# Other tiles for one block's sums, and an output whose stores are joined in pairs: a delta-rule attention with two dense layers on one core

## The chip, the core and the metric

The kernel runs on one core of one Trainium2 chip. The core has a matrix engine (TensorE, PE in the profile), three engines for elementwise work (VectorE or DVE, ScalarE or ACT, GpSimd or POOL), a SyncE (SP) that in this kernel only issues DMA transfers, and 16 DMA engines that carry the transfers. Each engine works through its own instructions in order and waits on semaphores for the others. The metric is the device time of one execution in microseconds; less is better. Three runs of the kernel before took 1066.85, 1068.50 and 1068.76 us (median 1068.5).

## The reference, cut to what matters

```python
def _attn_ref(q, k, v, beta):                  # (4, 8, 768, 48) each, beta (4, 8, 768)
    k_n = k / (norm(k) + 1e-6)
    for t in range(S):
        y[:, :, t] = q_t @ state
        state += b_t * outer(k_t, v_t - state.T @ k_t)

x = attn_out.transpose(0, 2, 1, 3).reshape(B * S, H * D)     # 3072 tokens x 384
h = x @ w_in;  x = elu(h) @ w_out                            # 384 -> 2048 -> 384, "layer 1"
h = x @ w2_in; x = (h * sigmoid(1.702 * h)) @ w2_out         # the same again, "layer 2"
```

The result is the float32 matrix of 3072 tokens by 384, token index `b * 768 + s`.

## The kernel before, in words

The 768 positions are cut into six blocks of 128 (p = 0 to 5, NP = 6). A block holds 128 positions of the four batches, 512 tokens (TB). The attention works in twelve chunks of 64 positions, two for each block, and is woven into the dense layers' loop.

The main loop in `schedule` has 192 units: layer 1 ("t") block by block with 16 units each (one unit is one slice of 128 of the 2048 hidden columns), then layer 2 ("n") in the same way. In a unit `up` (L573) makes nine matmuls into one PSUM bank `h`; ScalarE and VectorE apply the activation and split the result in a high and a low part, `gh` and `gl`; two units later (LAG = 2) `down_t` (L607, nine matmuls of 512 columns) or `down_n` (L618, twelve of 384) multiplies them by the second weight into accumulators in PSUM that stay open for the block's 16 units. Other work (attention steps, the conversion of the weights, the loading of the next block) hangs on tables `mid`, `end` and `fill` by unit number, which fixes every engine's order in the program text.

At the end of a block of layer 1, `end_t` copies the three accumulators (`acc`, 128 x 512 each) into two tiles of 128 x 768, `xo`: VectorE copies accumulator 0 and half of 1 into the first (L673), ScalarE accumulator 2 and the other half of 1 into the second (L671). SP stores both to a scratch tensor in DRAM, `x1d` (L653, L654). The next block's `down_t` needs the same three banks. A tile's tag names a ring of buffers: the tiles `xo` of blocks 0 to 4 have the tag "w" of pool `mp`, two buffers in all; those of block 5 the tag "xo" of pool `w2p`, also two. The ring "w" serves the weight conversion as well: each 128-row slice of weights comes as 64-bit words (`raw`, L527), ScalarE rescales them (L531), VectorE makes 32-bit words `w` of them (L538, L541), and ScalarE and VectorE split those in a high and a low part `wt` (L548, L552). The conversion of layer 2's weights runs through blocks 4 and 5 of layer 1. Pool `w2p` is opened in `attention_done`, in unit 79, the last of block 4; the sums of block 4 are copied out two units later.

In layer 2 a block begins with `x1_load`: SP loads `x1r` (768 KB) from `x1d` (L629), ScalarE (L634) and GpSimd (L635) split it in `xh` and `xl`. That is done one block ahead, in the units 2 to 12 of the block before. At a block's end `end_n` copies four accumulators (128 tokens x 384 each, w = 0 to 3) into tiles `on`, VectorE those of w = 0 and 2, ScalarE those of w = 1 and 3; each tile holds 64 positions of two batches, one batch in partitions 0 to 63, the other in 64 to 127, so it goes to two places in the output, 768 rows apart.

Of the kernel before, what the change touches and what calls it, by code (L numbers as in the profile page):

```python
# [17 lines left out]
B, H, S, D = 4, 8, 768, 48  # L18
DM = H * D
DFF = 2048  # L20
P = 128
NP = S // P
# [9 lines left out]
class Kernel:  # L32
# [607 lines left out]

    def end_t(self, p, c0, n, acc):

        pool, tag = (self.w2p, "xo") if p == NP - 1 else (self.mp, "w")
        d = self.x1d[p]
        halves = [pool.tile([P, 2 * DM], F32, name="xo", tag=tag, bufs=2) for _ in range(NK * n // (2 * DM))]
        if n == TB:
            x, y, n2 = *halves, n // 2
            self.evac(0, x[:, 0:n], acc[0])
            self.evac(1, y[:, n2:n2 + n], acc[2])
            self.evac(0, x[:, n:], acc[1][:, 0:n2])  # L650
            self.evac(1, y[:, 0:n2], acc[1][:, n2:n])
            d = d.rearrange("p k t -> p (k t)")
            self.nc.sync.dma_start(d[:, 0:2 * DM], x)  # L653
            self.nc.sync.dma_start(d[:, 2 * DM:], y)  # L654
        else:
            x = halves[0].rearrange("p (k t) -> p k t", k=NK)
            for c in range(NK):
                self.evac(c, x[:, c], acc[c])
            self.nc.sync.dma_start(d[:, :, c0:c0 + n], x)

    def end_n(self, p, acc):
        for w in range(NW):
            o = self.w2p.tile([P, DM], F32, name="on", tag="on", bufs=4)
            self.evac(w, o, acc[w])
            for ab in range(2):
                r = (2 * (w % 2) + ab) * S + p * P + 64 * (w // 2)
                self.nc.sync.dma_start(self.out[r:r + 64, :], o[64 * ab:64 * ab + 64])

    def evac(self, i, out, in_):
        if i % 2:  # L670
# [361 lines left out]
```

## Time and profile before

| what | value |
|---|---|
| median of the runs | 1068.5 us (1066.85 to 1068.76) |
| the profiled execution | 1067.46 us, of which the profile's span 1065.8 us |
| TensorE busy | 1001.8 us, 94% of the span |
| VectorE, ScalarE, GpSimd busy | 590.9, 451.4, 49.1 us |
| DMA | 68.41 MB, mean 64 GB/s |
| mean granted TensorE clock | 0.981 |

The span runs from the first to the last instruction of the profiled execution; 1.7 us of the execution's time lie around it. A busy engine is one that executes an instruction; waits, branches and the issuing of transfers do not count. "Idle before" is the time in which an engine stood still ahead of an instruction, with what released it. The granted clock is the share of full speed that the chip allowed TensorE: 1.00 is 2.4 GHz, 0.50 is 1.2 GHz.

### The profile page before, as it was taken

What the parts mean: (1) busy time and instruction counts of PE and PEld (TensorE: products, weight loads), DVE (VectorE), ACT (ScalarE), POOL (GpSimd) and SP (SyncE); (2) the same over time, 40 slices, a digit from 0 to 9 for tenths busy, and PEclk for the clock granted to TensorE, in tenths of its full rate; (3) what the DMA queues carried; (4) which work ended last, traced back from release to release, by engine and by line L of the source; (5) the groups of instructions that cost most, each with busy time, mean ns of one, the idle gap of its engine ahead of it and who ended that gap; (6) DMA issues with size and microseconds to landing.
All of it is one profiled execution on the core that took longest, in us unless ns stands there. A gap on an engine that the chain in (4) does not pass through costs nothing.

```text
span 1065.8 us, 26850 instructions
## 1 busy us (share of the span) xinstructions
PE 1001.8 (94%) x12136; PEld 855.6 (80%) x12136; DVE 590.9 (55%) x1021; ACT 451.4 (42%) x739; POOL 49.1 (5%) x65
## 2 busy tenths in 40 slices
PE   3576998989999999999999899999999999999997
PEld 3564776878887888888888788999999999999996
DVE  5449669846787677768434576653333333333332
ACT  1243575434445435544544567543333333332322
POOL 2000000000001000000000010000100001000000
PEclk9997999989999999999999999999999999999999
DMA  5555010401121221111001651002001020010101
GB/s 184 222 217 167 24 41 14 130 33 56 47 81 48 71 77 51 52 51 60 28 16 61 239 235 45 15 1 60 1 17 44 1 60 1 14 46 1 30 1 30
DMA packets 20562, 68.41 MB, mean 64 GB/s; under 512 B 3552, under 2 KB 6624, under 8 KB 20448
## 3 DMA queue, kind: packets, MB, share of 16 engines
q1 hardware_dynamic: 20448, 66.69, 18.8%
q8 instruction: 95, 1.56, 0.6%
q14 instruction: 19, 0.16, 0.0%
HBM read 57.25 MB, written 9.44 MB: 63 GB/s over the span
## 4 chain that ended last, share of the span: by engine, by line
PE 89%; DVE 5%; issue 2%; DMA 2%; ACT 1%; SPq 0%; ACTq 0%; DVEq 0%
PE h L573 37%; PE acc L607 18%; PE acc L618 10%; PE accn L618 9%; PE ps_w L362 2%; PE ps_w L474 2%; PE ps_w L459 1%; PE ps_b L392 1%; PE ps_w L188 1%; PE ps_b L407 1%; PE ps_w L423 1%; PE ps_w L440 1%; PE ps_b L315 1%; PE ps_b L323 1%; DVE w L541 1%
## 5 line engine op out<-in xcount | busy, mean ns | idle before, releaser
L573 PE MATMUL h<-xh,wt 128*128 128x512 f32 x1152 | 402.0, 403 | 9.8 <-DVE wt L552 6.1
L573 PEld LDWEIGHTS h<-xh,wt 128*128 128x128 f32 x1152 | 219.5, 191 | 57.0 <-DVE wt L552 7.4
L573 PE MATMUL h<-xl,wt 128*128 128x512 f32 x576 | 229.6, 399 | 0.0
L607 PE MATMUL acc<-gh,wt 128*128 128x512 f32 x576 | 198.6, 399 | 3.1 <-ACT xo L671 2.6
L595 ACT CAST gh<-t 128x512 fp32r<-128x512 f32 x192 | 119.2, 621 | 162.4 <-DVE t L586 106.1
L598 DVE TENSOR_TENSOR gl<-t,gh 128x512 fp32r<-128x512 f32 x192 | 138.4, 721 | 67.2 <-PE acc L618 28.9
L592 DVE TENSOR_TENSOR t<-t,h 128x512 f32<-128x512 f32 x96 | 66.1, 688 | 180.2 <-ACT t L589 180.1
L589 ACT ACTIVATE t<-h 128x512 f32<-128x512 f32 x96 | 57.3, 597 | 198.9 <-PE h L573 198.9
L607 PEld LDWEIGHTS acc<-gh,wt 128*128 128x128 f32 x576 | 109.2, 190 | 27.7 <-ACT xo L671 3.0
L573 PEld LDWEIGHTS h<-xl,wt 128*128 128x128 f32 x576 | 109.9, 191 | 19.2
L582 ACT ACTIVATE t<-h 128x512 f32<-128x512 f32 x96 | 57.4, 598 | 133.3 <-PE h L573 132.7
L607 PE MATMUL acc<-gl,wt 128*128 128x512 f32 x288 | 113.3, 394 | 0.0
L586 DVE SCALAR_TENSOR_TENSOR t<-t,h 128x512 f32<-128x512 f32 x96 | 65.5, 683 | 68.6 <-ACT t L583 68.2
L618 PE MATMUL acc<-wt,gh 128*128 128x384 f32 x384 | 98.4, 337 | 0.0
L618 PE MATMUL accn<-wt,gh 128*128 128x384 f32 x384 | 98.0, 336 | 0.0
L618 PEld LDWEIGHTS accn<-wt,gh 128*128 128x128 f32 x384 | 70.9, 188 | 5.5
L618 PEld LDWEIGHTS acc<-wt,gh 128*128 128x128 f32 x384 | 70.3, 188 | 2.8
L618 PE MATMUL acc<-wt,gl 128*128 128x384 f32 x192 | 64.9, 338 | 0.0
L618 PE MATMUL accn<-wt,gl 128*128 128x384 f32 x192 | 64.7, 337 | 0.0
L607 PEld LDWEIGHTS acc<-gl,wt 128*128 128x128 f32 x288 | 54.7, 190 | 10.2
L583 ACT ACTIVATE t<-t 128x512 f32<-128x512 f32 x96 | 60.6, 631 | 3.1
L635 POOL TENSOR_TENSOR xl<-x1r,xh 128x512 fp32r<-128x512 f32 x18 | 24.1, 1337 | 415.9 <-ACT xh L634 322.1
(142 smaller groups left out, 969.3 us busy)
## 6 DMA issues: line engine op xcount, KB each, us to landing
raw<-in_w SPq DMA_DIRECT2D x32, 768.0 KB, 10.7
kt<-in_kT SPq DMA_DIRECT2D x12, 512.0 KB, 4.7
x<-in_qT SPq DMA_DIRECT2D x24, 256.0 KB, 4.3
kg<-in_kT SPq DMA_DIRECT2D x10, 512.0 KB, 3.9
vn<-in_vn SPq DMA_DIRECT2D x12, 384.0 KB, 3.8
kn<-in_kn SPq DMA_DIRECT2D x12, 384.0 KB, 3.2
x1d<-xo SPq DMA_DIRECT2D x12, 384.0 KB, 2.8
x1r<-x1d SPq DMA_DIRECT2D x6, 768.0 KB, 4.5
```

What stands on the lines that cost most here:

```text
L362: pe.matmul(ps[hf][self.tok(k), 64 * u:64 * u + 64], g["kt"][r:r + D, 8 * hf + u, :], g["x"][k][r:r + D, 8 * hf + u, :], start=True, stop= ...
L573: nc.tensor.matmul(hps, wt[:, part, k * P:(k + 1) * P], src[:, k, c], start=(i == 0), stop=(i == 3 * NK - 1))
L582: nc.scalar.activation(out=t, in_=hps, func=AF.Relu, scale=-1.0)
L583: nc.scalar.activation(out=t, in_=t, func=AF.Exp, scale=-1.0)
L586: nc.vector.scalar_tensor_tensor(out=t, in0=t, scalar=-1.0, in1=hps, op0=ALU.add, op1=ALU.max)
L589: nc.scalar.activation(out=t, in_=hps, func=AF.Sigmoid, scale=1.702)
L592: nc.vector.tensor_tensor(out=t, in0=t, in1=hps, op=ALU.mult)
L595: nc.scalar.copy(gh, t)
L598: nc.vector.tensor_tensor(out=gl, in0=t, in1=gh.bitcast(F32), op=ALU.subtract)
L607: self.nc.tensor.matmul(acc[c], wt[:, part, DM + c * P:DM + (c + 1) * P], src, start=(m == 0 and i == 0), stop=(m == NM - 1 and i == 2),)
L618: self.nc.tensor.matmul(acc[w], src[:, c], wt[:, part, DM:2 * DM], start=(m == 0 and i == 0), stop=(m == NM - 1 and i == 2),)
L635: nc.gpsimd.tensor_tensor(out=xl[:, c, :], in0=st["raw"][:, c, :], in1=xh[:, c, :].bitcast(F32), op=ALU.subtract)
```

## The change

Three edits. The sums of block 4 (the fifth) use the tiles "xo" of pool `w2p`, as those of block 5 do, in place of the ring "w". Each tile `on` leaves in one transfer, whose output side is a view of two batches by 64 rows by 384 columns, in place of two transfers of 64 rows. In the last block the transfers of w = 1 and 3 are issued by ScalarE (`nc.scalar`) on its own queue, in place of SP.

```diff
     def end_t(self, p, c0, n, acc):
 
-        pool, tag = (self.w2p, "xo") if p == NP - 1 else (self.mp, "w")
+        pool, tag = (self.w2p, "xo") if p >= NP - 2 else (self.mp, "w")
         d = self.x1d[p]
...
             self.evac(w, o, acc[w])
-            for ab in range(2):
-                r = (2 * (w % 2) + ab) * S + p * P + 64 * (w // 2)
-                self.nc.sync.dma_start(self.out[r:r + 64, :], o[64 * ab:64 * ab + 64])
+
+            b, r = 2 * (w % 2), p * P + 64 * (w // 2)
+            to = self.out.rearrange("(b s) d -> b s d", b=B)[b:b + 2, r:r + 64, :]
+            (self.nc.scalar if p == NP - 1 and w % 2 else self.nc.sync).dma_start(to, o)
```

No engine's computing instructions change their order; lines behind the change move down by one. What changes is what the copies wait for, and the transfers. On ScalarE, around the end of block 4 (`xo_7814` is the second tile, acc1 and acc2 the accumulators; in brackets what an instruction waits for: another engine, or a transfer's queue, DMAHW), the order before is

```order
L531 ACTIVATE raw_7779<-raw_7779 128x768 [waits DMAHW4_49,DMAHW3_49,DMAHW5_49,DMAHW2_49,DMAHW6_49,DMAHW1_49,DMAHW7_49,DMAHW0_49,Pool_49]
L531 ACTIVATE raw_7781<-raw_7781 128x768 [waits DMAHW5_49]
L671 COPY xo_7814<-acc2_6885 128x512 [waits DMAHW1_49,DMAHW6_49,DVE_49,PE_49]
L671 COPY xo_7814<-acc1_6884 128x256
L595 CAST gh_7794<-t_7793 128x512
L582 ACTIVATE t_7834<-h_7824 128x512 [waits PE_49]
```

and the same place after the change is

```order
L531 ACTIVATE raw_7779<-raw_7779 128x768 [waits DMAHW4_49,DMAHW3_49,DMAHW5_49,DMAHW2_49,DMAHW6_49,DMAHW1_49,DMAHW7_49,DMAHW0_49,Pool_49]
L531 ACTIVATE raw_7781<-raw_7781 128x768 [waits DMAHW5_49]
L672 COPY xo_7814<-acc2_6885 128x512 [waits PE_49]
L672 COPY xo_7814<-acc1_6884 128x256 [waits DVE_49]
L595 CAST gh_7794<-t_7793 128x512
L582 ACTIVATE t_7834<-h_7824 128x512 [waits PE_49]
```

The first copy no longer waits for transfers, nor for VectorE; the second now waits for VectorE, whose half of the same bank comes first. On SP, from the first block's output to the end of the program, the order before is

```order
L667 DMA out<-on 64x384 x8
L629 DMA x1r<-x1d 128x1536
L667 DMA out<-on 64x384 x8
L629 DMA x1r<-x1d 128x1536
L667 DMA out<-on 64x384 x8
L629 DMA x1r<-x1d 128x1536
L667 DMA out<-on 64x384 x8
L629 DMA x1r<-x1d 128x1536
L667 DMA out<-on 64x384 x16
```

and after the change

```order
L668 DMA out<-on 2x64x384 x4
L629 DMA x1r<-x1d 128x1536
L668 DMA out<-on 2x64x384 x4
L629 DMA x1r<-x1d 128x1536
L668 DMA out<-on 2x64x384 x4
L629 DMA x1r<-x1d 128x1536
L668 DMA out<-on 2x64x384 x4
L629 DMA x1r<-x1d 128x1536
L668 DMA out<-on 2x64x384 x6
```

Half as many transfers stand ahead of each load, and the last two blocks have six on SP. The other two stand on ScalarE, at the end of its program, each behind the copy that fills its tile:

```order
L589 ACTIVATE t<-h 128x512
L595 CAST gh<-t 128x512
L672 COPY on<-acc_10876 128x384
L668 DMA out<-on 2x64x384
L672 COPY on<-acc_10878 128x384
L668 DMA out<-on 2x64x384
```

Before, ScalarE had the two copies there and no transfer between or behind them.

## Rows read from the trace of the kernel before

**Rows 1.** The page: busy time by engine (part 1), chain that ended last (part 4)

```profile
PE 1001.8 (94%) x12136; PEld 855.6 (80%) x12136; DVE 590.9 (55%) x1021; ACT 451.4 (42%) x739; POOL 49.1 (5%) x65
...
PE 89%; DVE 5%; issue 2%; DMA 2%; ACT 1%; SPq 0%; ACTq 0%; DVEq 0%
```

**Rows 2.** Waits of TensorE: line, waited for, us in total, times, longest

```profile
PE acc L607 <- ACT xo L671: 2.6, 1, 2.6
```

**Rows 3.** Stages: start:end, length, busy us by engine, PEclk, DMA share, GB/s

```profile
586.71:590.79 4.08, 4.08 (x20) 3.38 (x19) 0.14 (x1) 2.43 (x4) 0.00 (x0) 1.00 0.00 0
590.79:602.17 11.38, 8.26 (x29) 6.05 (x27) 5.96 (x10) 4.86 (x9) 0.00 (x0) 0.85 0.47 165
```

**Rows 4.** Timeline, end of block 4: start, us, engine, instruction, [idle before <-releaser]

```profile
590.11 1.68 ACT L531 ACTIVATE raw<-raw 128x768 f32<-128x768 f32 x2
...
591.01 0.56 DVE L538 TENSOR_SCALAR w<-raw 128x768 uint32<-128x768 uint32 x1 [4.17 <-ACT raw L531]
...
592.69 1.02 DVE L673 COPY xo<-acc 128x512 f32<-128x512 f32 x2
...
593.52 0.47 PE L607 MATMUL acc<-gh,wt 128*128 128x512 f32 x1 [0.53 <-DVE xo L673]
...
596.12 0.86 ACT L671 COPY xo<-acc 128x512 f32<-128x512 f32 x2 [4.33 <-DMA x1d<-xo]
...
597.04 0.50 PE L607 MATMUL acc<-gh,wt 128*128 128x512 f32 x1 [2.59 <-ACT xo L671]
...
599.76 0.56 DVE L538 TENSOR_SCALAR w<-raw 128x768 uint32<-128x768 uint32 x1 [5.19 <-DMA x1d<-xo]
```

**Rows 5.** Tile xo: instruction, count, ns min/median/max, first and last start

```profile
L673 DVE COPY xo<-acc x12: 414/550/685, 213.2 to 661.3; 128x512 f32<-128x512 f32 x6, 128x256 f32<-128x256 f32 x6
```

**Rows 6.** Timeline, last block's end

```profile
1058.16 0.48 ACT L671 COPY on<-acc 128x384 f32<-128x384 f32 x1 [3.19 <-PE acc L618]
1058.23 4.96 SPq L667 DMA_DIRECT2D out<-on  x8
...
1058.83 0.34 PE L618 MATMUL acc<-wt,gl 128*128 128x384 f32 x1
1059.21 0.48 ACT L671 COPY on<-acc 128x384 f32<-128x384 f32 x1 [0.56 <-PE acc L618]
```

**Rows 7.** Tile on, from 1057.5 us to the end

```profile
L667 SPq DMA_DIRECT2D out<-on x8: 466/570/593, 1058.2 to 1062.6; - x8
...
DMA to landing us min/median/max: 2.1/2.2/2.2
```

**Rows 8.** The page, DMA packets by size

```profile
DMA packets 20562, 68.41 MB, mean 64 GB/s; under 512 B 3552, under 2 KB 6624, under 8 KB 20448
```

**Rows 9.** DMA issues by kind: count, KB each, median us to landing

```profile
raw<-in_w SPq DMA_DIRECT2D x32, 768.0 KB, 10.7
...
out<-on SPq DMA_DIRECT2D x48, 96.0 KB, 2.2
beta<-in_beta SPq DMA_DIRECT2D x6, 16.0 KB, 4.5
```

**Rows 10.** Stages: x1d stores alone, weight loads, the tail's out stores

```profile
413.80:415.20 1.40, 1.40 (x7) 1.13 (x7) 1.40 (x3) 1.02 (x2) 0.00 (x0) 1.00 1.00 395
...
606.00:611.00 5.00, 5.00 (x23) 4.13 (x22) 3.63 (x5) 3.04 (x5) 0.00 (x0) 1.00 1.00 414
...
1060.00:1064.00 4.00, 0.00 (x0) 0.00 (x0) 0.00 (x0) 0.00 (x0) 0.00 (x0) 0.73 0.64 154
```

**Rows 11.** Timeline, layer 2: block 0's stores, next block's split, block 1

```profile
728.25 5.02 SPq L667 DMA_DIRECT2D out<-on  x8
...
747.87 0.61 ACT L634 CAST xh<-x1r 128x512 fp32r<-128x512 f32 x1
748.72 0.62 ACT L595 CAST gh<-t 128x512 fp32r<-128x512 f32 x1 [0.25 <-DVE t L592]
...
755.49 0.51 PE L618 MATMUL acc<-wt,gh 128*128 128x384 f32 x2
```

## The prediction, made before the result was known

> **What bounds the kernel now.** I read the page first. TensorE is busy 94% of the span and the chain that ended last runs over it for 89% [rows 1], so only two things can move the time: a place where TensorE stands still, or what follows its last matmul. The table of TensorE's waits gives one such place in the second half of the program, 2.6 us in L607 for ScalarE's copy `xo` in L671 [rows 2]; its longer waits lie in the attention's start, which the change leaves alone. The stage view gives that place's price: 586.71 to 590.79 is one unit of the loop (nine matmuls of `up`, nine of `down`) in 4.08 us with no gap, while 590.79 to 602.17 holds one and a half units (nine, nine, nine: 6.12 us at that pace) and takes 11.38, at a mean granted clock of 0.85 [rows 3]. So the place costs 11.38 - 6.12 = 5.26 us. The timeline tells why [rows 4]: VectorE copies accumulator 0 and half of 1 at 592.69, but ScalarE copies the rest only at 596.12, after 4.33 us idle "<-DMA x1d<-xo"; TensorE's next matmul into that bank starts at 597.04.
>
> At the other end, TensorE's last matmul starts at 1058.83 and the last copy `on` ends at 1059.21 + 0.48 = 1059.69, but the span ends at 1065.8: eight stores are issued one behind another on SP from 1058.23 to 1058.23 + 4.96 = 1063.19 [rows 6], the last at 1062.6, and each lands 2.1 to 2.2 us after its issue [rows 7]; from the last landing to the end it is 1065.8 - 1064.8 = 1.0 us. This tail of 6.1 us is what the second half of the change is about.
>
> **Part 1, other tiles for the fifth block's sums.** `xo` of block 4 leaves the tag "w", two tiles that the weight conversion also uses, for the two tiles "xo" of block 5. In the order, ScalarE's first copy loses its waits on DMA queues and VectorE and waits for TensorE alone; its second waits for VectorE. Nothing else moves there, and the two tiles are free: block 5 copies into them 68 us later (VectorE's last such copy at 661.3 [rows 5]). ScalarE is free at 590.11 + 1.68 = 591.79 [rows 4], so `acc2` is copied by about 592.4. Its half of `acc1` follows VectorE's half (592.69 + 1.02 = 593.71) and ends near 594.1. TensorE wants that bank after the three matmuls that start at 593.52, at 0.227 us each (4.08 / 18) 594.2: no second wait. The first, 0.53 us, stays, as VectorE still comes late to its copy (4.17 us idle for ScalarE's L531 [rows 4]). With the 2.59 us gone I expect no half-clock stretch either: the 0.85 of [rows 3] is 11.38 x 0.15 = 1.7 us lost, and followed that stop. Bounds of the gain: 2.6 us (the named wait alone) and 5.2 us; I take 5.26 - 0.53 - some 0.2 = **4.5 us**, since wait and clock belong to one event. What could be late next is the weight stream: VectorE's next L538 waited 5.19 us for the second half's store [rows 4] and does so no longer; SP's loads behind that store are issued some 2.8 us earlier while TensorE is 4.5 us earlier, so ScalarE may wait some 2 us for one, under the two units (8 us) by which `gh` runs ahead.
>
> **Part 2, joined stores.** Each pair of 64-row stores becomes one of 128 rows, so the issues fall from 48 [rows 9] to 24. Before the tail they lie beside a TensorE without gaps, and that saves nothing. In the tail the fourth store could be issued near 1059.8 in place of 1062.6. But the new store writes 2x64x384: two blocks of 64 rows, 768 rows apart in the output, outermost count 2. No transfer before has that form; all have 64 or 128 rows outermost. What I can read of these: the page has 3552 packets under 512 B [rows 8]; the six `beta` loads are 16 KB each, 128 rows of 128 B, together 768 packets; the other 2784 are 16 for each of the 174 transfers (the counts of the ten kinds in [rows 9] summed). I read them as one end mark from each of 16 DMA engines: a transfer of 64 or 128 rows is dealt out over all. How is one with an outermost count of 2 dealt out? If it goes by the outermost count, as 64 and 128 go into sixteen shares, there are two shares and two engines carry everything. The trace does not show it; the bounds are sixteen engines and two. I take two: the outermost count is what all 174 have in common, a multiple of 16, and the new form alone lacks it.
>
> The Trainium skill ("DMA: Bandwidth & Descriptors", section "Why a DMA increments its semaphore by 16 and not by 1") says that a transfer from SP or ACT runs on the largest number of engines, at most 16, that divides the outermost count of both its sides. By that rule it would be two; the 16 small packets a transfer agree with it for 64 and 128 rows, and no run here shows a smaller count.
>
> Price with two. The rate of one engine: loads of 6 KB rows keep all sixteen at share 1.00 with 414 GB/s, 25.9 each; stores of 3 KB rows from 128 partitions do 395 GB/s at 1.00, 24.7 each; the 64-row `out` stores 154 GB/s at 0.64, 15.0 each [rows 10]. A row of 1536 B thus takes 59, 62 or 102 ns; I take 64, next to the 128-partition store, for the joined one also reads 128 partitions. The last block's four stores are 512 rows; two engines get 256 rows each, and a second queue adds no engine: 256 x 64 ns = 16.4 us. A store that lands 2.2 us after its issue has four rows an engine, 0.4 us, in motion, so 1.8 us are fixed: 1058.23 + 1.8 + 16.4 + 1.0 = 1077.4. The tail grows by **11.6 us**.
>
> Earlier blocks: their stores take the same 16.4 us, unseen, but the next block's `x1r` load is issued right behind on SP, and on those two engines it comes after them: 728.25 + 1.8 + 16.4 = 746.5, then its 48 KB share at 26 GB/s, 1.9 us: 748.4. ScalarE's first L634 stands at 747.87 [rows 11], 0.5 us before. That is covered: the `gh` copied at 748.72 is read two units later, at 755.49 [rows 11], so the load may land up to 754.2 (6.3 us late, with 1.3 us for the two copies behind it) before TensorE waits. Cost 0; with rows slower than (754.2 - 1.9 - 1.8 - 728.25) / 256 = 87 ns that cover is gone, four times.
>
> **The sum.** Profiled span 1065.8 - 4.5 + 11.6 = 1072.9. The profiled execution took 1067.46, 1.7 more than its span: 1074.6. The median of the runs shown, 1068.5, is 1.0 above it: **1075.6 us**.
>
> **Rivals.**
> *Sixteen engines after all* (not slower). The store's rows go to all engines, as in all stores before. SP issues the first and third; ScalarE, behind its copies, the second and fourth. The second's issue (0.47 to 0.59 us, as SP's in the tail [rows 7]) follows the copy that ends at 1058.16 + 0.48 [rows 6], so it ends near 1059.2, when the last copy could start anyway; the fourth goes out at 1059.75, lands 2.2 to 2.7 later, and 1.0 more makes 1063.0 to 1063.5: 2.6 us won. 1065.8 - 4.5 - 2.6 = 1058.7, as a median 1061.4. For it: 174 of 174 transfers are spread so. Against: none of them has an outermost count below 64. It decides from about eight engines a store on: then 64 rows each, 4.1 us, fit into the time that the issues take now.
>
> The Trainium skill ("DMA: Bandwidth & Descriptors", section "Issuing engines are not separate DMA queues") says that issuing from several engines saves only the time of issuing. By it the second queue gains at most the issues of [rows 6] that stand one behind another, which is all that this rival wins; no run here shows a second queue.
>
> *Two engines at the slow pace*, 100 ns a row as in the 64-row stores. 25.6 us in place of 16.4, so the tail ends at 1086.6; the `x1r` loads land near 757.6, 3.4 us past TensorE's cover, in four blocks: 13 us, up to 20 if each stop brings the half clock (1.7 us) as the one of [rows 3] did. 1065.8 - 4.5 + 20.8 + 13 to 20 = 1095 to 1102; as a median about 1101. Against it: the rate of 128 partitions in [rows 10].
>
> *Two engines, and Part 1 gives nothing*: ScalarE's next wait (a weight load, or VectorE's order) stops TensorE for as long. 1080.1.
>
> *In between*: four to six engines share a store; then tail and Part 1 cancel, near 1068.
>
> **How the numbers follow.** Forecast 0.69; sixteen engines 0.13; slow pace 0.10; Part 1 void 0.06; in between 0.02. Within 0.2%, or 2.1 us, is what a measurement of this kernel can't tell from no change. Faster 0.13, same 0.02, slower 0.85. The range runs from 1071 (59 ns a row, Part 1 at its upper bound, a low run) to 1088 (rows of some 90 to 95 ns, their cover just gone); it leaves out the sixteen engines and most of the slow pace, 0.2 in all.
>
> **What would show it.** In the profile after: no "ACT xo <- DMA" wait near 593, the one and a half units from 590.79 in about 6.9 us, no half clock there. `out` in 24 issues that land 5 to 16 us after their issue; DMA share in the tail about 2/16 = 0.13 at 48 GB/s; packets under 512 B fewer by 24 x 16 + 24 x 14 = 720 (2832). The span ends about 17 us after the last copy. I am wrong if `out` lands in 2 to 3 us, or if TensorE waits in the second layer behind L634.

## The result, and the profile after

The changed kernel takes 1078.61 us (median of four runs, 1077.05 to 1080.03) against 1068.63 for the kernel before (four runs, 1066.85 to 1071.28): a ratio of 1.0092, 95% interval 1.0066 to 1.0118. It is slower by 0.92%, more than the 0.2% that can be told from no change.

Its profiled execution took 1077.05 us, with a span of 1075.3 against 1065.8 before. The two halves of the change are read one after the other. First comes the end of block 4, in the stages that answer to [rows 3]: the same columns (length, busy us by engine, PEclk, DMA share, GB/s), at the same two places of the program.

```profile
588.82:592.90 4.08, 4.08 (x20) 3.38 (x18) 0.14 (x1) 2.43 (x4) 0.00 (x0) 1.00 0.00 0
592.90:599.81 6.91, 6.38 (x29) 4.93 (x28) 6.49 (x11) 4.85 (x9) 0.00 (x0) 1.00 0.45 162
```

The one and a half units took 11.38 us and take 6.91; the granted clock stays at 1.00. The timeline there (start, us, engine, instruction, idle before it) answers to [rows 4]:

```profile
593.82 0.56 ACT L672 COPY xo<-acc 128x512 f32<-128x512 f32 x1
...
594.80 1.02 DVE L674 COPY xo<-acc 128x512 f32<-128x512 f32 x2
...
595.63 0.47 PE L607 MATMUL acc<-gh,wt 128*128 128x512 f32 x1 [0.53 <-DVE xo L674]
...
595.85 0.38 ACT L672 COPY xo<-acc 128x256 f32<-128x256 f32 x1 [1.47 <-DVE xo L674]
...
596.17 0.63 PE L607 MATMUL acc<-gh,wt 128*128 128x512 f32 x2
...
596.60 0.55 DVE L538 TENSOR_SCALAR w<-raw 128x768 uint32<-128x768 uint32 x1
```

ScalarE copies `acc2` before VectorE begins, and its half of `acc1` right behind VectorE's; TensorE still waits the 0.53 us and no longer the 2.59; VectorE's next L538 waits for no store. Then comes the end of the program, the stretch of [rows 6]:

```profile
1055.79 0.48 ACT L672 COPY on<-acc 128x384 f32<-128x384 f32 x1 [3.19 <-PE acc L618]
1055.86 1.55 SPq L668 DMA_DIRECT2D out<-on  x2
...
1056.30 1.16 ACTq L668 DMA_DIRECT2D out<-on  x1
...
1056.46 0.34 PE L618 MATMUL acc<-wt,gl 128*128 128x384 f32 x1
1057.55 0.48 ACT L672 COPY on<-acc 128x384 f32<-128x384 f32 x1 [1.28 <-PE acc L618]
1058.06 0.53 ACTq L668 DMA_DIRECT2D out<-on  x1
```

All four stores are issued by 1058.6, sooner behind the last copy than before, yet the span ends at 1075.3, 17.3 us after that copy. What runs in these 17 us is in the stage view:

```profile
1060.00:1072.00 12.00, 0.00 (x0) 0.00 (x0) 0.00 (x0) 0.00 (x0) 0.00 (x0) 0.55 0.13 50
```

Nothing computes; the mean share of the 16 DMA engines is 0.13, that is 2 of 16, and they move 50 GB/s, 25 each. The page counts the packets:

```profile
DMA packets 19843, 68.40 MB, mean 64 GB/s; under 512 B 2833, under 2 KB 5905, under 8 KB 19729
...
q10 hardware_dynamic: 260, 0.39, 0.1%
```

There are 719 fewer small packets than in [rows 8]: 24 transfers less, and 2 end marks instead of 16 for each of the 24 that remain (384 + 336 = 720; the page has one packet more on queue q14, 20 instead of 19). The queue that ScalarE used, q10, shows it alone: two stores of 128 rows are 256 packets, and 4 more.

In the earlier blocks the stretch of [rows 11] now reads, on SP and on ScalarE:

```profile
725.88 7.39 SPq L668 DMA_DIRECT2D out<-on  x4
733.38 3.67 SPq L629 DMA_DIRECT2D x1r<-x1d  x1
```

```profile
746.19 0.62 ACT L634 CAST xh<-x1r 128x512 fp32r<-128x512 f32 x1 [0.60 <-DMA x1r<-x1d]
```

The load of the next block comes 0.60 us late for ScalarE, and TensorE does not wait for it.

To compare all kernels, the same points are taken in each trace: the first matmul of `up` at block 4's end (590.79 before), the first of `down` one and a half units later (602.17), TensorE's last matmul, and the end of the span. The table has the first point's time and then the differences, in us; the last column is called the tail.

| kernel | to block 4's end | one and a half units | to TensorE's last matmul | from there to the end |
|---|---|---|---|---|
| before | 590.79 | 11.38 | 456.66 | 6.92 |
| changed | 592.90 | 6.91 | 456.65 | 18.86 |
| e1_tiles_only | 594.98 | 6.89 | 456.65 | 6.93 |
| e2_joined_sp | 596.28 | 6.93 | 456.65 | 18.61 |
| e3_two_queues_64 | 594.45 | 6.93 | 456.65 | 5.63 |
| e4_batch_rows | 593.76 | 6.91 | 456.65 | 3.83 |
| e5_62_rows | 595.65 | 6.95 | 456.65 | 18.77 |
| e6_joined_mid | 592.10 | 6.93 | 456.65 | 7.01 |
| e7_stores_only | 592.81 | 12.48 | 456.68 | 18.86 |
| e8_127_rows_mid | 594.57 | 6.93 | 504.20 | 3.89 |
| e9_before_again | 593.98 | 11.42 | 456.66 | 6.93 |
| e10_batch_rows_sp | 592.78 | 6.97 | 456.65 | 3.82 |

The change is the difference of the last three columns: 6.91 - 11.38 = -4.47 and 18.86 - 6.92 = +11.94, together +7.5 us.

### The profile page after: what moved, and what is told of

Its sections match the earlier page's. It is cut to its first block, busy times and chain, and to the rows that moved or that the text cites. A ratio compares the mean times of both kernels' runs of the same rounds, so it can differ in the third digit from the quotient of the medians.

```text
span 1075.3 us, 26818 instructions
## 1 busy us (share of the span) xinstructions
PE 1001.9 (93%) x12136; PEld 856.0 (80%) x12136; DVE 592.4 (55%) x1021; ACT 451.6 (42%) x739; POOL 49.5 (5%) x65
## 4 chain that ended last, share of the span: by engine, by line
PE 88%; DVE 5%; issue 2%; DMA 1%; ACT 1%; SPq 0%; ACTq 0%
PE h L573 37%; PE acc L607 18%; PE accn L618 9%; PE acc L618 9%; PE ps_w L362 2%; PE ps_w L474 2%; PE ps_w L459 1%; PE ps_w L188 1%; PE ps_b L392 1%; PE ps_b L407 1%; PE ps_w L423 1%; PE ps_w L440 1%; PE ps_b L323 1%; PE ps_b L315 1%; DVE w L541 1%
## 5 line engine op out<-in xcount | busy, mean ns | idle before, releaser
L607 PE MATMUL acc<-gh,wt 128*128 128x512 f32 x576 | 199.2, 400 | 0.5 <-DVE xo L674 0.5
L607 PEld LDWEIGHTS acc<-gh,wt 128*128 128x128 f32 x576 | 109.7, 190 | 24.9 <-issue 0.9
L607 PE MATMUL acc<-gl,wt 128*128 128x512 f32 x288 | 113.8, 395 | 0.0
L607 PEld LDWEIGHTS acc<-gl,wt 128*128 128x128 f32 x288 | 55.0, 191 | 10.4
```

The source lines that it names most:

```text
L607: self.nc.tensor.matmul(acc[c], wt[:, part, DM + c * P:DM + (c + 1) * P], src, start=(m == 0 and i == 0), stop=(m == NM - 1 and i == 2),)
```

## The experiments

The theory: a store goes to as many DMA engines as its outermost count allows, so 2x64x384 goes to two, and the last four stores take 256 rows an engine; Part 1 (the tiles) is a gain of 4.5 us that this covers up. Rivals: the second queue costs the time; a store of 128 partitions is slow in itself; the step of 768 rows between the batches binds it; Part 1 is given back. Ratios are to the kernel before on the same chip. The edit of e1 is shown against the kernel before, those behind it against the changed kernel; `...` marks lines left out.

**e1_tiles_only**, the first edit alone.

```diff
-        pool, tag = (self.w2p, "xo") if p == NP - 1 else (self.mp, "w")
+        pool, tag = (self.w2p, "xo") if p >= NP - 2 else (self.mp, "w")
```

> Part 1 alone: block 4's sums through the two tiles of block 5, the 48 stores of 64 rows as before. Theory (the stop of 2.59 us, the half-clock stretch behind it and what lies between are one event): 4.5 us less than the kernel before on the same chip, no ScalarE wait on a store near 593, one and a half units in about 6.9 us. Rival (the stop is given back later, by a wait for weights in layer 1's last block or in layer 2): within 1 us of before, with a new TensorE wait behind 597.

Measured: 1066.05 against 1070.58 us, ratio 0.9951 (0.9932 to 0.9970); the stretch is 6.89 us, everything behind it as before. Of TensorE's waits in L607 one is left:

```profile
PE acc L607 <- DVE xo L673: 0.5, 1, 0.5
```

The gain is kept to the end (4.5 us by the medians), so the rival falls.

**e2_joined_sp**, the changed kernel without the second queue.

```diff
-            (self.nc.scalar if p == NP - 1 and w % 2 else self.nc.sync).dma_start(to, o)
+            self.nc.sync.dma_start(to, o)
```

> The changed kernel with all 24 joined stores on SP, no second queue. Theory (two DMA engines carry a store with an outermost count of 2, so the last four stores take 256 rows an engine whoever issues them): as the changed kernel, within 1 us, 7 to 10 us over before; 2832 or 2833 packets under 512 B; DMA share 0.13 in the tail. Rival (the second queue, used for the first time in the tail, is what costs the 11 us): back to about 4 to 7 us under before.

Measured: 1079.87 us, ratio 1.0082 (1.0054 to 1.0110), 2832 packets under 512 B. The tail's stage:

```profile
1063.00:1075.00 12.00, 0.00 (x0) 0.00 (x0) 0.00 (x0) 0.00 (x0) 0.00 (x0) 0.60 0.13 50
```

Two engines again, and a tail of 18.61 us against 18.86: whoever issues the stores, the 12 us stay. The second queue is worth at most the 0.25 us between the two, and not in its favour.

**e3_two_queues_64**, stores of 64 rows, two queues.

```diff
...
+            for ab in range(2):
+                r = (2 * (w % 2) + ab) * S + p * P + 64 * (w // 2)
+                on = self.nc.scalar if p == NP - 1 and w % 2 else self.nc.sync
+                on.dma_start(self.out[r:r + 64, :], o[64 * ab:64 * ab + 64])
```

> Part 1 and the second queue, but stores of 64 rows as before (outermost count 64): in the last block ScalarE issues the four of w = 1 and 3. Theory: sixteen engines a store; the last store is issued near 1060.9 of before's scale in place of 1062.6, so the tail shrinks by about 1.7 us and the whole is 6 us under before. Rival (a second queue costs time of its own): slower than Part 1 alone.

Measured: 1064.51 us, ratio 0.9937 (0.9914 to 0.9960); the tail is 5.63 us, 1.3 shorter than before, 0.4 less than expected. Two issues stand ahead of ScalarE's last copy and hold it back:

```profile
1057.88 1.20 ACTq L669 DMA_DIRECT2D out<-on  x2
...
1059.20 0.48 ACT L673 COPY on<-acc 128x384 f32<-128x384 f32 x1 [1.35 <-PE acc L618]
```

1.35 us idle there, against 0.56 in [rows 6].

**e4_batch_rows**, stores of 128 rows with an outermost count of 128. The attention's `out` writes its columns by batch, so that a tile `on` holds 128 consecutive rows of the output.

```diff
-                src = ps[i][:, 0:HB].rearrange("p (k t) -> p k t", k=NK)
-                dst = slice(d, d + P)
-                act.copy(xh[:, :, dst], src)
...
+                src = ps[i][:, 0:HB].rearrange("p (k b t) -> p k b t", k=NK, b=2)
+                to = [x.rearrange("p k (b h t) -> p k b h t", b=B, h=2)[:, :, 2 * i:2 * i + 2, c % 2, :] for x in (xh, xl)]
+                act.copy(to[0], src)
...
+            r = w * S + p * P
+            (self.nc.scalar if p == NP - 1 and w % 2 else self.nc.sync).dma_start(self.out[r:r + P, :], o)
```

> Part 1, the second queue and 24 stores of 128 rows, but with an outermost count of 128: the attention writes a block's 512 columns batch by batch, so that a tile holds 128 consecutive rows of the output. Theory (it is the outermost count of 2, not the joining): sixteen engines a store, packets under 512 B = 3552 - 24 x 16 = 3168, the last store issued at 1059.75 lands after 2.2 to 2.7 us, the tail is 2.6 us shorter than before, the whole 7 us under before. Rival (a store of 128 partitions or 192 KB is slow in itself, or ScalarE's queue is): some 7 us over before, as the changed kernel.

Measured: 1062.70 us, ratio 0.9931 (0.9907 to 0.9955). Issue times (ns min/median/max) and landing (us) of its stores:

```profile
L666 SPq DMA_DIRECT2D out<-on x22: 332/384/443, 726.7 to 1057.8; - x22
...
DMA to landing us min/median/max: 1.9/2.0/2.5
```

```profile
DMA packets 20178, 68.40 MB, mean 64 GB/s; under 512 B 3168, under 2 KB 6240, under 8 KB 20064
```

3168 is 16 end marks a store. Each tile is as large as in the changed kernel, has as many partitions and goes out on the same queue, and yet the tail is 3.83 us instead of 18.86. So neither joining nor the queue is slow in itself; it is the output's side, which now has an outermost count of 128 in place of 2 and no step between batches (e5 tells these two apart). All sixteen engines work in this tail:

```profile
1057.60:1059.80 2.20, 0.06 (x1) 0.00 (x0) 0.13 (x1) 0.48 (x1) 0.00 (x0) 1.00 0.99 353
```

353 GB/s at a share of 0.99 are 22 an engine.

**e5_62_rows**, stores of 64 rows on SP as before, with the last block's cut in 62 rows and 2; no step between batches is left.

```diff
...
+                for u, n in ((0, 62), (62, 2)) if p == NP - 1 else ((0, 64),):
+                    self.nc.sync.dma_start(self.out[r + u:r + u + n, :], o[64 * ab + u:64 * ab + u + n])
```

> Part 1, all stores on SP with 64 rows as before, but in the last block each is cut in one of 62 rows and one of 2. Every store is contiguous in the output; no batch step of 768 rows is left. Theory in its narrow form (the number of engines is the largest up to 16 that divides the outermost count): 62 goes by 2, so two engines carry 256 rows each again; end marks 3552 - 128 + 16 x 2 = 3456; tail 18 to 28 us after TensorE's last matmul (64 to 102 ns a row), 12 to 21 longer than Part 1 alone. Rival A (the rows are dealt out over sixteen engines whenever there are at least sixteen): only the 8 more issues count, tail about 12 us, some 5 longer than Part 1 alone. Rival B (it is the step between the two batches that binds a store to two engines): as rival A.

Measured: 1077.86 us against 1070.67, ratio 1.0066 (1.0041 to 1.0091); tail 18.77 us.

```profile
1064.00:1072.00 8.00, 0.00 (x0) 0.00 (x0) 0.00 (x0) 0.00 (x0) 0.00 (x0) 0.50 0.13 50
```

```profile
DMA packets 20466, 68.41 MB, mean 63 GB/s; under 512 B 3456, under 2 KB 6528, under 8 KB 20352
```

3456 is what the narrow form has: 62 goes to two engines though it has more than sixteen rows, and a share of 0.13 says the same. So what counts is what divides the outermost count, and the batch step is not needed for it. The Trainium skill's rule ("DMA: Bandwidth & Descriptors", section "Why a DMA increments its semaphore by 16 and not by 1"), the largest number up to 16 that divides it, agrees with all the end marks counted here: 16 for 64 and 128, 2 for 2 and 62, and 1 for 127 and 1 in e8. These counts do not tell it from a rule that goes by powers of two alone; a count like 12 or 100 would, and none was run.

**e6_joined_mid**, joined stores in blocks 0 to 4 alone.

```diff
...
+            if p < NP - 1:
+                b, r = 2 * (w % 2), p * P + 64 * (w // 2)
+                self.nc.sync.dma_start(self.out.rearrange("(b s) d -> b s d", b=B)[b:b + 2, r:r + 64, :], o)
+                continue
...
```

> Part 1; joined stores (outermost count 2) in blocks 0 to 4, stores of 64 rows on SP in the last. Theory: the slow stores of the earlier blocks lie beside TensorE and their delay of the next load is covered: within 1 us of Part 1 alone, 4.5 us under before; TensorE's stretch from block 4's end to its last matmul 456.65 us as in all others; ScalarE waits 0.4 to 0.6 us at the first L634 of four blocks; packets under 512 B 3552 - 40 x 16 + 20 x 2 = 2952. Rival (half of the 10 us comes from these blocks): 2 us or more over Part 1 alone.

Measured: 1065.49 us, ratio 0.9957 (0.9941 to 0.9974), 2952 packets under 512 B as forecast, and ScalarE's waits, which stand in one row:

```profile
ACT xh L634 <- DMA x1r<-x1d: 2.0, 4, 0.6
```

As Part 1 alone: the slow stores of five blocks cost nothing.

**e7_stores_only**, the second and third edit alone (the line of e1 back).

> Part 2 alone (joined stores, second queue), block 4's sums through the ring w as before. Theory (the two parts add): 4.5 us over the changed kernel, 11 to 12 over before; the stretch of one and a half units at block 4's end 11.4 us, the tail 18.7 us behind TensorE's last matmul. Rival (Part 1's gain depends on what the stores do): within 2 us of the changed kernel.

Measured: 1082.27 us, ratio 1.0102 (1.0065 to 1.0139), 11.6 us over before by the medians. The wait of [rows 4] is back and the tail is 18.86 us, but the one and a half units take 12.48 us, 1.1 more than before, with a granted clock of 0.73 there instead of 0.85 [rows 3]:

```profile
592.81:605.29 12.48, 9.36 (x28) 6.86 (x27) 6.79 (x11) 4.86 (x9) 0.00 (x0) 0.73 0.52 190
```

In the stages the parts add, give or take that 1.1. The whole times alone do not show it: this ratio and the changed kernel's 1.0092 lie in each other's intervals.

**e8_127_rows_mid**, e4 with the stores of blocks 0 to 4 cut in 127 rows and 1.

```diff
...
+            for u, k in ((0, P),) if p == NP - 1 else ((0, 127), (127, 1)):
+                on.dma_start(self.out[r + u:r + u + k, :], o[u:u + k])
```

> The kernel with 128 consecutive rows a tile (outermost count 128), but in blocks 0 to 4 each store is cut in one of 127 rows and one of 1. Theory: 127 has no divisor up to 16 but 1, so one engine carries 4 x 128 rows, 32.8 us at 64 ns, and the next x1r load waits for its share there: it lands 1.8 + 32.8 + 1.9 = 36.5 us after the block's first store, 10 us beyond the point from which TensorE waits (26 us after it). Four stops of 10 us, 12 with the half clock behind each: 40 to 48 us over the same kernel with whole stores; end marks 3552 - 768 + 40 + 64 = 2888. Rival (a load does not queue behind stores on an engine, or the cover is longer than I read): within 3 us of the kernel with whole stores.

Measured: 1111.59 us, ratio 1.0380 (1.0344 to 1.0417), and 504.20 us where the others have 456.65. The 2888 packets under 512 B are what one end mark for each of the 40 cut stores gives, and the DMA share behind block 0's end is 0.07, one engine of sixteen, at 26 GB/s:

```profile
729.00:745.00 16.00, 16.00 (x82) 14.61 (x81) 5.84 (x9) 4.88 (x8) 0.00 (x0) 1.00 0.07 26
```

What waits, in us in total, times, longest:

```profile
PE acc L617 <- ACT gh L594: 18.0, 2, 9.0
PE accn L617 <- ACT gh L594: 17.9, 2, 9.0
```

```profile
ACT xh L633 <- DMA x1r<-x1d: 61.8, 4, 15.5
```

One of the four, in time:

```profile
727.57 25.29 SPq L668 DMA_DIRECT2D out<-on  x8
752.95 0.93 SPq L628 DMA_DIRECT2D x1r<-x1d  x1
```

```profile
762.79 0.62 ACT L633 CAST xh<-x1r 128x512 fp32r<-128x512 f32 x1 [15.51 <-DMA x1r<-x1d]
```

The load is there 35.2 us after the block's first store (36.5 expected), and TensorE stops for 9.0 us (10 expected): it would have waited from 26.2 us after the store, against 26 expected. The four stops make 35.9 of the 47.5 us; the other 11.6, 2.9 a block, lie behind them, where the granted clock is 0.64 for 8 us:

```profile
764.10:772.00 7.90, 7.53 (x26) 6.54 (x27) 3.99 (x5) 3.05 (x6) 1.94 (x2) 0.64 0.00 0
```

**e9_before_again**, the kernel before, unchanged, for a second profile.

> The kernel before, once more, for a second profile of it. All the profiles since reach block 4's end 1.3 to 5.5 us later than the one that the prediction was read from (592.1 to 596.3 against 590.79), though no edit stands ahead of that place. Theory: the attention's start varies by that much from execution to execution, by where the half-clock stretches fall, and the first profile was an early one; this one comes at 592 to 596, then a stretch of 11 to 12.5 us, 456.65 us, and a tail of 6.9. Rival: the edits do cost time ahead of block 4's end; then this one comes at 590 to 591 again.

Measured: 1070.70 us in its one run. It comes to block 4's end at 593.98, 3.2 us later than in the first profile, and has 11.42, 456.66 and 6.93 us behind that. No edit is needed for that difference. A large part of it can be placed. These are the 16 us from 240 to 256 (TensorE's busy us and matmuls, PEclk, DMA share, GB/s), in the first profile and then in this one:

```profile
240.00:256.00 16.00, 15.81 (x341) 1.00 0.10 28
240.00:256.00 16.00, 16.00 (x274) 0.80 0.10 28
```

The first execution had the full clock there and did 341 matmuls, this one a mean of 0.80 and 274. Why the first kept the full clock is open.

**e10_batch_rows_sp**, e4 on SP alone.

> As the kernel with 128 consecutive rows a tile, but all 24 stores on SP. Theory: with sixteen engines a store and an issue of 0.33 to 0.44 us the fourth store goes out right behind its copy on either queue; the tail stays within 0.3 us of 3.8 and the whole within 0.2% of the kernel with two queues. Rival (the second queue is worth something of its own): the tail is 1 us longer or more.

Measured: 1062.80 us, ratio 0.9938 (0.9913 to 0.9963) beside 1062.70 and 0.9931 for e4; tail 3.82 us. With stores of 128 rows on sixteen engines the second queue is worth nothing. The Trainium skill says the same of several issuing engines ("DMA: Bandwidth & Descriptors", section "Issuing engines are not separate DMA queues"): they share the DMA engines and save only the time of issuing. The runs agree: with the eight longer issues of 64 rows the second queue saved 1.3 us (e3), with four short ones nothing (e10).

## Why the prediction was right, point by point

*The place at block 4's end.* Right in cause and size: one event, wait and clock together, worth 4.47 us (4.5 predicted), and the first 0.53 us stay. e1 shows that it is not given back.

*Two engines.* Right, and it decided the sign. It was a choice between two bounds, argued and not read, for the trace before could not show it. The end marks in the page and the share of 0.13 show it now, and e4 with e5 shows that the count alone makes 15.0 us of the tail. The landings 5 to 16 us after the issue, which were to show it too, can't be read: the changed kernel's profile gives none.

*The price of the tail.* Predicted +11.6 us, measured +11.94. The terms of the sum can be read in the changed kernel's stages, from the first issue to the end of the span:

```profile
1055.86:1057.00 1.14, 0.94 (x6) 0.61 (x4) 0.56 (x1) 0.41 (x1) 0.00 (x0) 1.00 0.00 0
1057.00:1060.00 3.00, 0.00 (x0) 0.00 (x0) 0.00 (x0) 0.48 (x1) 0.00 (x0) 1.00 0.13 29
1060.00:1074.00 14.00, 0.00 (x0) 0.00 (x0) 0.00 (x0) 0.00 (x0) 0.00 (x0) 0.54 0.13 50
1074.00:1075.30 1.30, 0.00 (x0) 0.00 (x0) 0.00 (x0) 0.00 (x0) 0.00 (x0) 0.50 0.00 0
```

The rows take 17.0 us where the working had 16.4, that is 66 ns each instead of 64; the fixed part is 1.1 us ahead of them and 1.3 behind, 2.4 instead of 2.8. These are two small misses of opposite sign. The 66 ns are a mean: the two engines move 29 GB/s in the first 3 us and 50 behind that (61 ns a row), and what holds them at first was not tried.

The pace was read from the right row, but the reason given for it, that 128 partitions are read, is not shown. In e5 stores of 62 partitions on two engines also run at 25 GB/s an engine, so 128 partitions are not needed; in e4 stores of 128 partitions on sixteen engines run at 22, so sixteen engines alone do not slow them. Of the forms that ran, only the stores of 64 rows on sixteen engines are slower, at 15.0 in [rows 10]; why was not tried.

*The earlier blocks.* Right: the load came 0.60 us late where 0.5 was predicted, without cost. e8 put the limit of that cover where the working had it (26.2 against 26 us after the first store).

*The slow pace, sixteen engines, Part 1 void.* The first falls with 25 GB/s an engine in every profile with two engines, the second with the end marks, the third with e1. What the second rival described exists all the same: e4 is that tail, 3.1 us under before where the rival's working had 2.6.

*The time itself.* 1078.61 against 1075.6. The difference of the two medians is 10.0 us where 7.1 was forecast and the stages give 7.5; the interval (7.1 to 12.6 us) holds all three. The changed kernel's profile has 2.1 us of it ahead of block 4's end, where no edit stands, and e9 shows the kernel before losing 3.2 us there in another execution. As far as the runs show, the term that was too low is the sum's base: one profiled execution, an early one, and a median of three runs. In the experiments, on three chips, the kernel before has medians of 1070.12 to 1070.67 us over 16 to 19 runs; chips may differ, so this supports it and does not prove it.

## What to carry to other kernels

Before transfers are joined, look at the outermost count of both sides: a view that puts a 2 in front of 64 rows halves the number of issues and leaves two DMA engines of sixteen. If that count can be kept at a multiple of 16, here by having the producer write the columns in the output's row order, the same joining is a gain: the tail is 3.83 us where Part 1 alone has 6.93, and the whole 0.9931 of the time before where the changed kernel has 1.0092. Slow transfers cost nothing in the middle of this kernel as long as the load queued behind them had slack (e6), and 12 us a block once it had none (e8); so look for their price at the end and in that slack.

## What the runs showed beyond that

The issuing engine itself is held by transfers with few engines. Four joined stores keep SP for 7.39 us, and the `x1r` load behind them takes 3.67 us to issue. Before, it took 0.54:

```profile
733.37 0.54 SPq L629 DMA_DIRECT2D x1r<-x1d  x1
```

With one engine a store (e8) SP stands in eight issues for 25.29 us. On ScalarE the first joined store's issue took 1.16 us and put off the last copy by 0.7 us (1.28 us idle against 0.56), which the prediction's tail had at zero; e2, which issues nothing there, has a tail 0.25 us shorter. Stores of 128 rows on sixteen engines are issued by SP in 0.33 to 0.44 us (e4), those of 64 rows in 0.47 to 0.59 [rows 7].
